# One DMA queue, a guard time behind each transfer, and another home for the attention outputs in a fused window-attention and SwiGLU kernel

## The chip, the cores and the metric

The kernel runs on one core of one Trainium2 chip. The metric is the device time of one execution in microseconds (us), as the median of the runs shown. A profiled execution gives the trace; its own time is listed beside it. Engines: TensorE (PE; its weight loads are PEld), VectorE (DVE), ScalarE (ACT), GpSimd (POOL) and SyncE (SP). DMAs are issued by SP, and in this kernel also by ScalarE.

## What is computed

```python
xn = layernorm(x)                                   # x: 2048 x 512
q, k, v = split(xn @ wqkv)                          # 32 heads of 16
p = softmax(q @ k.T / 4, where 0 <= i - j < 256)    # a sliding window of 256 keys
s = (p @ v) @ wo
f = (silu(xn @ w_gate) * (xn @ w_up)) @ w_down      # inner width 1792
out = x + s * silu(f)
```

All tensors are fp32. The kernel computes each dense product as three products of split operands (high x high, high x low, low x high), so every weight and every activation is written twice, as a rounded high part and a low rest.

## The kernel before, in words

**Tiles and stages.** The 2048 tokens are four chunks (c) of 512. A chunk's x is normalised, transposed by TensorE (`x_turn`, line 356, for chunk 0; `xt_turn`, line 485, for the others) and split into `xn[c % 2]`, two sets of buffers that chunks use in turn. The dense work of a chunk is a list of units, each with a 256 KB or 192 KB weight tile that is loaded (tile `wr`), split by ScalarE (`wh`, line 439) and GpSimd (`wl`, line 443), and used by TensorE in two 64-row halves side by side (all at line 478): `Proj` (q and k of two head groups, out `a`), `Values` (`vp`), `GateUp` (`g` and `u`, 14 a chunk), `Down` (`d`, four quarters, two halves each) and `Wo`, the output projection (`s`, two halves). Attention goes by 32 units u of one chunk and four heads: q and k come back from DRAM (`load_qk`, line 928), `max_pair` (line 957) forms scores `b` whose row maxima VectorE takes (`m`, line 978), `max_turn` (line 998) transposes the maxima and ScalarE negates them (`ms`, line 1019), a DMA writes them into a row of the q tile (`put`, line 1025), and the scores `c` are formed again with that row as an extra term (line 1116), so that ScalarE's exponential (`p`, line 1078) needs no subtraction. GpSimd masks `p`, and `pv_visit` (line 1133) multiplies with v, which carries a column of ones for the denominator. The result `ev` is stored to DRAM (`od`).

**Denominators.** When two units of a head group are stored, `reciprocals` (line 854) reads the denominators back (`den<-od`), VectorE inverts them (line 866) and a DMA writes them to DRAM (`rd<-den`). `o_prep` (line 877) then loads the outputs (`o<-od`) and the broadcast reciprocals (`r<-rd`), multiplies on GpSimd and splits into `oh`, the input of `Wo`. Before the change these copies take four of the eight buffers of the hidden activations (`hidden`, line 639, given back when `Wo` is done at line 803); only the last chunk's go into x buffers. `o_prep` opens with the end of a `Down` quarter (lines 721 to 730, sets `o_open` and `h_open`).

**What sets the order.** The program is written out by a planner that runs while the kernel is built; on the chip every engine follows its own list in order and waits on semaphores. The planner keeps a clock for TensorE's two halves (`issue`, line 1307) and a queue of jobs for each of VectorE, ScalarE, GpSimd and SP (letters V, S, G, D). `do` (line 110) adds a job with its earliest time, cost and slack; `pump` (line 136) gives each engine, when it is free, the able job with the least due time. `dma` (line 118) is such a job: at most eight are in flight (`lanes`), the landing is reckoned as the queue's backlog at 230 KB a us (`stream_at`) plus LAND = 3.5 us, and `then` is called with that time, from which everything that uses the data is planned. A DMA with `own=True` is issued by ScalarE (`e="S"`) and reckoned to land SHORT = 2.8 us after its issue, whatever the backlog. These are `put` of `ms`, and `fetch` and `back` of `reciprocals`. The dense units stand in one list made by `dense_order` (line 1222); attention visits have due times in units of attention, s = work / PACE - LEAD with PACE = 17.6 us, and are put between dense products when due and ready (lines 1394 to 1441). A `Wo` unit whose s is below 8 (c + 1) + OUT counts as early (variable `late`, line 1264), and a `Proj` may then go ahead of it.

Of the kernel before, what the change touches and what calls it, by code (L numbers as in the profile page):

```python
# [38 lines left out]
PCAP = 7168  # L39
NSL = 14  # L40
NWB = 10
WSL = 4.0
SPARE = 3
LAG = 7
# [4 lines left out]
MM = 0.2315  # L49
PACE = 17.6  # L50
LEAD = 1.1
OUT = 2.0
STEP = 0.05
LAND = 3.5
SHORT = 2.8


@with_exitstack
def tile_window_attention_swiglu_gate(
# [55 lines left out]
    lanes = [0.0] * 8  # L115
    stream_at = [0.0]

    def dma(ready, fn, then=None, slack=0.5, kb=256, can=None, e="D", own=False):
        def begun_at(t):
            if own:  # L120
                done = t + SHORT
            else:
                stream_at[0] = max(stream_at[0], t) + kb / 230.0
                done = stream_at[0] + LAND
            lanes.append(done)
            lanes.pop(0)
            if then:
                then(done)

        do(e, ready, 0.5, fn, begun_at, slack, lambda: lanes[0] <= now[0] and (can is None or can()), 0.0)  # L130

# [348 lines left out]


    def xt_ready(c, k):
        return latest([*(normed.get((c, t)) for t in range(4)), bank_time(rb_free, 2)])

    def xt_turn(c, k):
# [93 lines left out]
    class GateUp(Stationary):  # L579
# [7 lines left out]

        def done(self, i, pb, t, free):
            c, fb = self.c, self.fb
            if i == 0:  # L590
                def tanh():
                    self.th = take(f"th{c}_{fb}")
                    self.y = take(f"y{c}_{fb}")
                    nc.scalar.activation(self.th, pb, AF.Tanh, scale=0.5)

                def one():
                    nc.vector.scalar_tensor_tensor(
                        self.y, self.th, 1.0, pb, op0=ALU.add, op1=ALU.mult
                    )
                    give(self.th)  # L600

                def after_one(t):
                    free(t)
                    self.ty = t

                do("S", t, 0.5, tanh, lambda t: do("V", t, 0.61, one, after_one), can=room(2))
                return

            def product():
                self.h = take(f"h{c}_{fb}")  # L610
                nc.vector.scalar_tensor_tensor(
                    self.h, self.y, 0.5, pb, op0=ALU.mult, op1=ALU.mult
                )
                give(self.y)
                hid[c, fb] = hidden(f"hh{c}_{fb}")

            def high():
                nc.scalar.activation(hid[c, fb][:, 0, :], self.h, AF.Copy)

            def low():  # L620
                hl = hid[c, fb]
                nc.gpsimd.tensor_tensor(hl[:, 1, :], self.h, f32(hl[:, 0, :]), op=ALU.subtract)
                give(self.h)

            def after_product(t):
                free(t)
                do("S", t, 0.52, high, after_high, 1.0)

            def after_high(t):
                do("G", t, 1.24, low, lambda t: hready.__setitem__((c, fb), t), 1.0)  # L630

            do("V", t, 0.61, product, after_product, can=lambda: self.ty is not None and len(slots) >= 1 and hfree)

    hid = {}
    hready = {}
    hfree = [f"hr{i}" for i in range(NHID)]
    htag = {}
# [67 lines left out]
    class Down(Moving):  # L705
# [15 lines left out]
        def ended(self):  # L721
            for f in range(self.f0, self.f1):
                hid_release(hid.pop((self.c, f)))
            for n in range(2):
                if self.q == 2 + n:
                    h_open.add((self.c, n))
                if self.q == (2 if self.c < NCH - 1 else 0):
                    o_open.add((self.c, n))
                    for k in range(2):
                        o_prep(self.c, 2 * n + k)  # L730


        def done(self, i, pb, t, free):
            c, q, hf = self.c, self.q, self.hf
# [36 lines left out]
    class Wo(Moving):  # L771
# [28 lines left out]
        def done(self, i, pb, t, free):  # L800
            c, hf = self.c, self.hf
            p2 = pb.rearrange("p (t n) -> p t n", t=2)
            if hf == 1 and i == 1 and c < NCH - 1:
                for k in range(KC):
                    hid_release(oraw.pop((c, k)))
            finish(c, hf, i, p2, t, free)

    xr = {}
# [34 lines left out]


    ot = {}
    oraw = {}
    oready = {}
    o_open = set()
    h_open = set()
    od_at = {}  # L850
    rd_at = {}
    begun = set()
# [1 line left out]
    def reciprocals(c, k):  # L854
        t = latest(od_at.get(8 * c + 2 * k + n) for n in range(2))
        if t is None:
            return
        hd = slice(8 * k, 8 * k + 8)
        box = []

        def fetch():
            box.append(sb(f"den{c}_{k}", [P, 32], F32, "den", 2))
            move(box[0], od[c, hd, DH, :].rearrange("h (a n) -> h a n", n=32), nc.scalar)

        def rec():
            nc.vector.reciprocal(box[0], box[0])

        def back():
            move(rd[c, hd].rearrange("h (a n) -> (h a) n", n=32), box[0], nc.scalar)

        def landed_back(t):
            rd_at[c, k] = t
            o_prep(c, k)

        dma(t + 0.5, fetch, lambda t: do("V", t + 0.5, 0.3, rec, lambda t: dma(t + 0.3, back, landed_back, 0.5, 16, e="S", own=True)), 1.0, 16, e="S", own=True)

    def o_prep(c, k):
        if (c, k // 2) not in o_open or (c, k) not in rd_at or (c, k) in begun:
            return
        begun.add((c, k))  # L880
        hd = slice(8 * k, 8 * k + 8)
        box = []
        last = c == NCH - 1

        def fetch_o():
            box.extend(take(f"{n}{c}_{k}") for n in "or")
            move(box[0], od[c, hd, :DH, :])

        def fetch_r():
            move(box[1], rd[c, hd, :].unsqueeze(1).to_broadcast([8, DH, TC]))  # L890

        def mul():
            nc.gpsimd.tensor_tensor(box[0], box[0], box[1], op=ALU.mult)
            give(box[1])

        def high():
            if not last:
                t = hidden(f"oh{c}_{k}")
                oraw[c, k] = t
                ot[c, k] = [t[:, s, :] for s in range(2)]  # L900
            else:
                ot[c, k] = [xn[(c - 1) % 2][s][:, k, :] for s in range(2)]
            nc.scalar.activation(ot[c, k][0], box[0], AF.Copy)

        def low():
            nc.gpsimd.tensor_tensor(ot[c, k][1], box[0], f32(ot[c, k][0]), op=ALU.subtract)
            give(box[0])

        def then_o(t):
            dma(now[0], fetch_r, then_r, 0.0, 500)  # L910

        def then_r(t):
            do("G", t, 1.24, mul, then_mul, 1.0)

        def then_mul(t):
            do("S", t, 0.52, high, lambda t: do("G", t, 1.24, low, lambda t: oready.__setitem__((c, k), t), 0.5), 0.5,
               lambda: last or ((c, k // 2) in h_open and hfree))

        dma(max(now[0], rd_at[c, k]), fetch_o, then_o, 0.5, 256, room(2 + (0 if last else SPARE)))

# [77 lines left out]
    def max_turn(u, r):  # L998
        if r == 0:
            mtp[u] = [*bank(rb_free, f"mt{u}"), None]  # L1000
        pb, tag, _ = mtp[u]

        def go():
            nc.tensor.matmul(
                pb[:MW, R * r : R * r + R], mts[u % 2][half(r), :], ident[half(r), half(r)],
                is_transpose=True, start=True, stop=True,
            )

        if r == 0:
            def after(t):  # L1010
                mtp[u][2] = t

            extra[0].append((128, go, lambda t: do("V", t, 0.09, lambda: handover(pb), after, -1.0)))
            return
        box = []

        def neg():
            box.append(sb(f"ms{u}", [16, P], F32R, "ms", 2))
            nc.scalar.activation(box[0], pb[:16, :P], AF.Copy, scale=-1.0)

        def after_neg(t):
            rb_free[tag] = t
            dma(t - 0.17, put, lambda t: ms_at.__setitem__(u, t), -3.0, 8, e="S", own=True)

        def put():
            move(qs[u % 3][48 : 113 : 64], box[0], nc.scalar)

        extra[1].append((128, go, lambda t: do("S", t, 0.25, neg, after_neg, -1.0)))


# [191 lines left out]
    def dense_order():  # L1222
# [8 lines left out]
        for c in range(NCH):  # L1231
# [12 lines left out]
            gu(2, 3)  # L1244
            if c:
                wos(c - 1)
            gu(4, 5)
            dn(c, 0)
            gu(6, 7, 8)
            dn(c, 1)  # L1250
            if c < NCH - 1:
                gu(9, 10, 11, 12)
# [9 lines left out]
        while timed or ffn:  # L1262
# [5 lines left out]
            elif late and early and s > 8 * early[0][1].c - 2.4:  # L1268
                timed.remove(early[0])
                u = early[0][1]  # L1270
            else:
                u = ffn.pop(0)
            order.append(u)
# [32 lines left out]

    def issue(r, cols):
        front[0] = max(front[0], clock[r])
        clock[r] = front[0] + cols * 0.000444 + 0.004

    def next_mm(r):
        if extra[r]:
# [167 lines left out]
```

## Time and profile before

| | before |
|---|---|
| runs | 898.25, 899.52, 896.02 us |
| median | 898.25 us |
| profiled execution: its own time | 894.56 us |
| its span | 892.8 us |
| mean granted TensorE clock | 0.987 |
| DMA traffic | 139.60 MB, mean 156 GB/s |

The span is the time from the first to the last instruction of the profiled execution. Busy times are sums over an engine; matmuls are pipelined, so a busy TensorE isn't TensorE at its peak, and what counts is where it waits and at what clock it runs. A row of waits reads: the engine and line that waited, what ended the wait, then total us, times and the longest. A row of the chain reads: start, length, what; the chain is followed back from the last instruction, at each step to what released it. SPq and ACTq are the instruction queues of SyncE and ScalarE, in which DMAs are issued. Names such as `q<-ms` mean a tile written from another.

### The profile page before, as it was taken

The numbers are of one execution on the slowest core, as the hardware profiler recorded it, in microseconds if no ns is written. First come the engines' busy times: TensorE is split into PE (matmuls) and PEld (weight loads), VectorE is DVE, ScalarE is ACT, GpSimd is POOL, SyncE is SP. The second block draws the span as 40 slices with busy tenths as digits, with TensorE's granted clock in tenths as the row PEclk, the third lists the DMA queues.
The fourth block names the chain that finished last, engine by engine and source line by source line (L and its number), as shares of the span: only waits on it lengthen the run. The fifth ranks groups of instructions, "written<-read, shape, count | busy, mean of one in ns | idle before, by whom it ended". The sixth has DMA issues, their size and how long they took to land.

```text
span 892.8 us, 29790 instructions
## 1 busy us (share of the span) xinstructions
PE 867.6 (97%) x11966; PEld 802.2 (90%) x11966; DVE 504.4 (56%) x1663; ACT 480.4 (54%) x948; POOL 626.4 (70%) x904
## 2 busy tenths in 40 slices
PE   9999999999999799999899999999999999999997
PEld 8899888998899798989899989989899999998897
DVE  4454476654755466666547676566655576544234
ACT  3455465655655346655466546655655574555531
POOL 4766386858676567867678678757768697878780
PEclk9999999999999999999989999999999999999999
DMA  7765757467657873676748887385666866843441
GB/s 191 172 167 134 184 121 190 120 174 169 173 134 181 243 177 84 145 168 134 208 97 194 189 185 197 89 208 112 155 150 178 190 151 176 207 125 106 112 117 48
DMA packets 69485, 139.60 MB, mean 156 GB/s; under 512 B 14546, under 2 KB 23250, under 8 KB 69348
## 3 DMA queue, kind: packets, MB, share of 16 engines
q1 hardware_dynamic: 64004, 136.39, 63.1%
q8 instruction: 94, 1.54, 0.8%
q10 hardware_dynamic: 5344, 1.31, 0.8%
q14 instruction: 43, 0.35, 0.2%
HBM read 107.74 MB, written 29.62 MB: 154 GB/s over the span
## 4 chain that ended last, share of the span: by engine, by line
PE 82%; DMA 13%; DVE 1%; issue 1%; POOL 1%; SPq 1%; ACT 1%; ACTq 0%; DVEq 0%; POOLq 0%
PE d L478 16%; PE u L478 15%; PE g L478 15%; PE a L478 11%; PE pv L1153 7%; PE c L1116 5%; PE s L478 4%; PE b L970 4%; PE vp L478 4%; DMA q<-ms 3%; DMA q<-qkd 2%; DMA den<-od 2%; DMA wr<-wgu 2%; DMA xt<-x 1%; DMA qkd<-qkh 1%; PE warm L240 1%
## 5 line engine op out<-in xcount | busy, mean ns | idle before, releaser
L443 POOL TENSOR_TENSOR wl<-wr,wh 128x512 fp32r<-128x512 f32 (+3 forms) x262 | 310.5, 1200 | 73.5 <-ACT wh L439 63.8
L978 DVE CUSTOM_DVE_ANT_0 jk<-b,maskb 128x384 bf16<-128x384 f32 (+2 forms) x512 | 271.7, 531 | 125.2 <-PE b L970 61.0
L1078 ACT ACTIVATE p<-c 128x512 f32<-128x512 f32 (+2 forms) x384 | 198.6, 569 | 154.2 <-PE c L1116 133.1
L478 PE MATMUL d<-wh,hh 64*128 64x256 f32 x1792 | 266.8, 278 | 0.0
L478 PEld LDWEIGHTS d<-wh,hh 64*128 64x128 f32 x1792 | 229.4, 185 | 1.4 <-issue 0.6
L478 PE MATMUL d<-wl,hh 64*128 64x256 f32 x896 | 207.0, 277 | 0.0
L439 ACT ACTIVATE wh<-wr 128x512 fp32r<-128x512 f32 (+3 forms) x262 | 144.9, 591 | 38.4 <-POOL wl L443 8.2
L478 PE MATMUL g<-xh,wl 64*128 64x512 f32 x448 | 165.1, 399 | 0.0
L478 PE MATMUL g<-xh,wh 64*128 64x512 f32 x448 | 164.8, 400 | 0.0
L478 PE MATMUL g<-xl,wh 64*128 64x512 f32 x448 | 164.7, 399 | 0.0
L478 PE MATMUL u<-xl,wh 64*128 64x512 f32 x448 | 164.6, 399 | 0.0
L478 PE MATMUL u<-xh,wl 64*128 64x512 f32 x448 | 164.4, 399 | 0.0
L478 PE MATMUL u<-xh,wh 64*128 64x512 f32 x448 | 164.2, 398 | 0.0
L1090 POOL TENSOR_SCALAR_AFFINE_SELECT p<-p 128x256 f32<-128x256 f32 x256 | 102.0, 411 | 82.4 <-ACT p L1078 81.9
L478 PEld LDWEIGHTS d<-wl,hh 64*128 64x128 f32 x896 | 148.5, 185 | 0.4
L970 PE MATMUL b<-k,q 48*128 48x384 f32 (+2 forms) x512 | 121.0, 333 | 6.5 <-ACT p L1078 4.0
L1094 POOL TENSOR_SCALAR_AFFINE_SELECT p<-p 128x256 f32<-128x256 f32 x224 | 92.3, 412 | 37.9 <-ACT p L1078 36.6
L1116 PE MATMUL c<-q,k 49*128 49x128 f32 (+2 forms) x704 | 108.2, 305 | 8.8 <-DMA q<-ms 8.7
L1116 PEld LDWEIGHTS c<-q,k 49*128 49x128 f32 x704 | 88.2, 190 | 12.9 <-issue 8.1
L478 PE MATMUL a<-xh,wh 64*128 64x512 f32 x256 | 97.2, 396 | 0.1
L478 PE MATMUL a<-xh,wl 64*128 64x512 f32 x256 | 96.6, 395 | 0.0
L478 PE MATMUL a<-xl,wh 64*128 64x512 f32 x256 | 96.4, 394 | 0.0
(116 smaller groups left out, 2088.4 us busy)
## 6 DMA issues: line engine op xcount, KB each, us to landing
wr<-wgu SPq DMA_DIRECT2D x112, 256.0 KB
k<-qkd SPq DMA_DIRECT2D x48, 192.0 KB
wr<-wqk SPq DMA_DIRECT2D x32, 256.0 KB
qkd<-qkh SPq DMA_DIRECT2D x32, 256.0 KB
qkd<-qkl SPq DMA_DIRECT2D x32, 256.0 KB
q<-qkd SPq DMA_DIRECT2D x64, 128.0 KB
wr<-wdn SPq DMA_DIRECT2D x32, 256.0 KB
od<-ev SPq DMA_DIRECT2D x32, 256.0 KB
```

Of the source, the lines that this page charges most:

```text
L240: nc.tensor.matmul(wbank[:, : rhs.shape[-1]], warm, rhs, start=True, stop=True)
L439: nc.scalar.activation(wtile[j][0][pr, a:b], raw[pr, a:b], AF.Copy)
L443: nc.gpsimd.tensor_tensor(lo[pr, a:b], raw[pr, a:b], f32(hi[pr, a:b]), op=ALU.subtract)
L478: return nc.tensor.matmul(pb, a, b, start=first, stop=last, skip_group_check=True)
L970: nc.tensor.matmul(pb[:, :n], qs[u % 3][r : r + 48, p, qb * P : (qb + 1) * P], ks[u % 3][r : r + 48, p, lo : lo + n], start=True, stop=True,)
L978: nc.vector.tensor_tensor_reduce(junk[:, :n], pb[:, :n], maskb[:, 3 * P - n :], 1.0, -3.0e38, ALU.add, ALU.max, m[:, col : col + 1],)
L1078: nc.scalar.activation(t[:, h, :], pc[:, :n], AF.Exp, scale=DH ** -0.5)
L1090: nc.gpsimd.affine_select(s, s, [[0, 2], [1, P]], ALU.is_ge, 0.0, base=0, channel_multiplier=-1)
L1094: nc.gpsimd.affine_select(s, s, [[0, 2], [-1, P]], ALU.is_gt, 0.0, base=0, channel_multiplier=1)
L1116: nc.tensor.matmul(pc[:, at0 : at0 + w], ks[u % 3][r : r + 49, p, k0 : k0 + P], qs[u % 3][r : r + 49, p, qb * P : qb * P + w], start=(i == ...
L1153: nc.tensor.matmul(pbs[r][0][32 * j : 32 * j + 32, q0:q1], vt[half(r), (4 * c + kb) % VT, VW * (4 * g + j) : VW * (4 * g + j) + 32], t[hal ...
```

## The change

- `dma` loses `own` and SHORT: every DMA after the first x loads is issued by SP and reckoned with the common backlog. `reciprocals` and `put` lose their ScalarE issues.
- `then` of a DMA gets its landing time plus GUARD = 1.5 us, once the landing lies past 15 us. The lanes are still freed at the time without it.
- The attention outputs of every chunk c before the last go into `xn[c % 2]`, the x buffers of the chunk itself, once its last gate-up unit is done (`x_used`); the transposes of chunk c + 2 wait for `Wo` of chunk c (`x_free`). The last chunk's still go into the other set. No hidden buffers are taken, and `h_open` and `oraw` are gone.
- `o_prep` opens at gate-up unit OPEN = 11 (4 in the last chunk) instead of at the end of a `Down` quarter.
- Order: gate-up unit 6 goes ahead of the first `Down` quarter; OUT is 2.4 instead of 2.0; and where a `Wo` is early, the gate-up unit behind its two halves may go ahead of it.
- The planner reckons a 512-column product at 0.2339 us instead of 0.2313.

```diff
+OPEN = 11
-OUT = 2.0
+OUT = 2.4
-SHORT = 2.8
+GUARD = 1.5
...
-    def dma(ready, fn, then=None, slack=0.5, kb=256, can=None, e="D", own=False):
+    def dma(ready, fn, then=None, slack=0.5, kb=256, can=None, e="D"):
         def begun_at(t):
-            if own:
-                done = t + SHORT
-            else:
-                stream_at[0] = max(stream_at[0], t) + kb / 230.0
-                done = stream_at[0] + LAND
+            stream_at[0] = max(stream_at[0], t) + kb / 230.0
+            done = stream_at[0] + LAND
             lanes.append(done)
             lanes.pop(0)
             if then:
-                then(done)
+                then(done + (GUARD if t > 15.0 else 0.0))
...
     def xt_ready(c, k):
+        if c not in x_free:
+            return None
...
             c, fb = self.c, self.fb
+            if i == 1 and fb == FB - 1:
+                x_used.add(c)
+            if i == 0 and fb == (OPEN if c < NCH - 1 else 4):
+                o_open.add(c)
+                for k in range(KC):
+                    o_prep(c, k)
...
+    x_used = set()
+    x_free = {0, 1}
...
                 hid_release(hid.pop((self.c, f)))
-            for n in range(2):
-                if self.q == 2 + n:
-                    h_open.add((self.c, n))
-                if self.q == (2 if self.c < NCH - 1 else 0):
-                    o_open.add((self.c, n))
-                    for k in range(2):
-                        o_prep(self.c, 2 * n + k)
...
-            if hf == 1 and i == 1 and c < NCH - 1:
-                for k in range(KC):
-                    hid_release(oraw.pop((c, k)))
+            if hf == 1 and i == 1:
+                x_free.add(c + 2)
...
-            move(box[0], od[c, hd, DH, :].rearrange("h (a n) -> h a n", n=32), nc.scalar)
+            move(box[0], od[c, hd, DH, :].rearrange("h (a n) -> h a n", n=32))
...
-            move(rd[c, hd].rearrange("h (a n) -> (h a) n", n=32), box[0], nc.scalar)
+            move(rd[c, hd].rearrange("h (a n) -> (h a) n", n=32), box[0])
...
-        dma(t + 0.5, fetch, lambda t: do("V", t + 0.5, 0.3, rec, lambda t: dma(t + 0.3, back, landed_back, 0.5, 16, e="S", own=True)), 1.0, 16, e="S", own=True)
+        dma(t, fetch, lambda t: do("V", t, 0.3, rec, lambda t: dma(t, back, landed_back, 0.5, 16)), 1.0, 16)
...
-        if (c, k // 2) not in o_open or (c, k) not in rd_at or (c, k) in begun:
+        if c not in o_open or (c, k) not in rd_at or (c, k) in begun:
...
         def high():
-            if not last:
-                t = hidden(f"oh{c}_{k}")
-                oraw[c, k] = t
-                ot[c, k] = [t[:, s, :] for s in range(2)]
-            else:
-                ot[c, k] = [xn[(c - 1) % 2][s][:, k, :] for s in range(2)]
+            ot[c, k] = [xn[(c - last) % 2][s][:, k, :] for s in range(2)]
...
-               lambda: last or ((c, k // 2) in h_open and hfree))
+               lambda: last or c in x_used)
...
-            dma(t - 0.17, put, lambda t: ms_at.__setitem__(u, t), -3.0, 8, e="S", own=True)
+            dma(t, put, lambda t: ms_at.__setitem__(u, t), -3.0, 8)
...
-            move(qs[u % 3][48 : 113 : 64], box[0], nc.scalar)
+            move(qs[u % 3][48 : 113 : 64], box[0])
...
-            gu(4, 5)
+            gu(4, 5, 6)
             dn(c, 0)
-            gu(6, 7, 8)
+            gu(7, 8)
...
+            elif late and isinstance(ffn[2], GateUp):
+                u = ffn.pop(2)
             else:
                 u = ffn.pop(0)
...
-        clock[r] = front[0] + cols * 0.000444 + 0.004
+        clock[r] = front[0] + cols * 0.000453 + 0.002
```

More of the change, by code (lines that the diff above doesn't have):

```diff
@@ L845, in tile_window_attention_swiglu_gate @@
     ot = {}
-    oraw = {}
     oready = {}
     o_open = set()
-    h_open = set()
     od_at = {}
```

## The prediction

> **What bounds the kernel now.** I read the page's totals first, then TensorE's own waits, then the granted clock around them, then the chain through the gaps.
>
> ```profile
> span 892.8 us, 29790 instructions
> PE 867.6 (97%) x11966; PEld 802.2 (90%) x11966; DVE 504.4 (56%) x1663; ACT 480.4 (54%) x948; POOL 626.4 (70%) x904
> ```
>
> TensorE is the bound: 97% busy, with every other engine at 70% or less. Its work is not changed by the diff (same matrix products, another order), so the change can only win or lose time in which TensorE waits or runs at a lower clock. TensorE's waits, all of them over 0.15 us after the start-up (columns: total us, times, longest):
>
> ```profile
> PE c L1116 <- DMA q<-ms: 8.7, 5, 3.1
> PE b L970 <- ACT p L1078: 4.0, 2, 3.3
> PE b L970 <- DVE m L978: 2.4, 2, 2.1
> PE mt L1004 <- DVE m L978: 2.0, 1, 2.0
> PE s L478 <- issue: 1.7, 1, 1.7
> ```
>
> These add to 8.7 + 4.0 + 2.4 + 2.0 + 1.7 = 18.8 us. The second cost stands in the clock column of the windows (PEclk, third from the right):
>
> ```profile
> 309.70:316.50 6.80, 5.44 (x30) 4.78 (x32) 3.07 (x10) 3.29 (x6) 3.50 (x6) 0.50 0.74 194
> 446.20:453.00 6.80, 5.75 (x40) 5.78 (x42) 1.73 (x5) 1.68 (x3) 3.05 (x5) 0.50 0.96 202
> 524.70:528.10 3.40, 3.40 (x29) 3.40 (x27) 1.82 (x5) 1.09 (x2) 0.75 (x3) 0.50 0.91 186
> 695.40:698.80 3.40, 3.40 (x21) 3.40 (x19) 0.15 (x1) 1.52 (x5) 2.43 (x5) 0.50 0.71 201
> ```
>
> TensorE ran 6.8 + 6.8 + 3.4 + 3.4 = 20.4 us at half clock, which costs half of that, 10.2 us. Where do the waits come from? The chain, in order of time (start, length, what):
>
> ```profile
> 280.33 7.62 DMA q<-qkd
> ...
> 288.02 5.12 DMA q<-ms
> ...
> 441.41 5.71 DMA q<-ms
> ...
> 447.25 0.91 PE c L1116 x4
> ...
> 521.83 1.83 issue
> ...
> 795.41 9.03 DMA den<-od
> ```
>
> All but the one at 521.83 end in small transfers that ScalarE (ACT) issues: the negated row maxima (ms into q) and the softmax denominators (den); their reciprocals (rd) are the third kind. c starts 0.13 us after its ms has landed (441.41 + 5.71 = 447.12). den landed 9.03 us after its issue, at 804.44; VectorE (DVE) waits for it to form the reciprocals, and the row maxima m, for which b and mt wait, stand behind on VectorE. ScalarE is in order, so a DMA that cannot be issued yet also holds the exponentials behind it:
>
> ```profile
> 303.39 1.15 ACT L439 ACTIVATE wh<-wr 128x512 fp32r<-128x512 f32 x2
> 309.18 0.64 ACTq L98 DMA_DIRECT2D den<-od  x1
> 309.92 1.09 ACT L1078 ACTIVATE p<-c 128x512 f32<-128x512 f32 x2 [5.38 <-DMA xt<-x]
> ...
> 437.73 0.27 ACT L1019 ACTIVATE ms<-mt 16x128 fp32r<-16x128 f32 x1 [0.42 <-PE g L478]
> 441.41 0.52 ACTq L98 DMA_DIRECT2D q<-ms  x1
> ```
>
> From 304.54 to 309.18, 4.6 us, ScalarE did nothing but wait to issue the denominators; the exponentials came at 309.92, and TensorE waited for them (the 3.3 us of b for p). At 438.00 the maxima were ready, issued 3.4 us later and landed 5.7 us after that. Each time the planner had counted on 2.8 us after the issue (SHORT) and not on the traffic of the other queue.
>
> **The change part by part.** *All DMAs on SP.* ScalarE loses these issues (instruction, count, min/median/max in ns):
>
> ```profile
> L98 ACTq DMA_DIRECT2D q<-ms x32: 505/530/1142, 52.8 to 811.8; - x32
> L98 ACTq DMA_DIRECT2D den<-od x16: 627/632/640, 108.3 to 843.2; - x16
> L98 ACTq DMA_DIRECT2D rd<-den x16: 320/321/353, 114.2 to 849.5; - x16
> ```
>
> 32 x 0.53 + 16 x 0.63 + 16 x 0.32 = 32 us of issuing, plus the holds. ScalarE is busy 54%, so the 32 us are worth nothing by themselves; the holds are. The wait of b for p (4.0 us) goes, and the half-clock stretch at 309.7 behind it (6.8 us, so 3.4). SP takes the 32 us, and has room on average, as its own waits show:
>
> ```profile
> SPq L98 <- POOL wl L443: 107.8, 38, 8.5
> ```
>
> For 107.8 us it stands only until GpSimd has freed a weight buffer. But SP is in order too and now takes the holds over: queued behind a waiting ms, den or rd are the weight loads and the next unit's q and k, and for those TensorE has no wait today.
>
> *Slack.* The planner now reckons with LAND + GUARD = 3.5 + 1.5 = 5.0 us for these transfers plus the backlog of the queue, where it had 2.8 and none. That moves the readers later in every engine's fixed order, which is what the waits of c for ms (8.7) and of DVE's m (2.4 + 2.0) lack: the ms transfers above took 5.1 and 5.7 us, the den transfer 9.0. For ms the allowance grows by 2.2 us and the longest wait is 3.1, so a leftover of 0.9 at most if the transfer itself keeps its length. It will not quite: in the same burst q<-qkd on SP took 7.6 us where ms on ACT took 5.1, 2.5 longer, and in the burst around 441 two of SP's issues lie 3.3 us apart, so a transfer that comes in between waits half of that on average, some 1.6:
>
> ```profile
> 440.09 0.47 SPq L98 DMA_DIRECT2D wr<-wdn  x1
> 443.38 0.34 SPq L98 DMA_DIRECT2D od<-ev  x1
> ```
>
> So the bounds of this term are all (13.1 us) and less than nothing (the transfer lengthens by 2.5, the issue by 1.6, the allowance by 2.2: each wait grows by 1.9, five times 9.5 us). The backlog that is now counted decides, since it is largest just where the waits are; I take 70%: 9.2 us. Of the half-clock stretches at 446 and 695 (3.4 + 1.7 us lost) likewise 70%, 3.6. Longer reckoning also lets attention fall behind in a burst; dense products fill TensorE meanwhile, and this cover exists until the dense work runs short at the end, which it doesn't (below).
>
> *Heads' outputs in the x buffers.* The copies wait for the chunk's last gate-up instead of for free hidden buffers; the transposes of chunk c+2 now wait for the output projection of chunk c. The windows of s, and of the transposes (line 496), hold the tightest case, chunk 0 and chunk 2 (busy us and count after the comma: PE first):
>
> ```profile
> 265.00:303.00 38.00, 23.67 (x192) 22.55 (x192) 2.96 (x8) 1.00 0.79 214
> 303.00:338.00 35.00, 0.00 (x0) 0.00 (x0) 0.90 0.71 159
> 338.00:359.00 21.00, 2.42 (x32) 2.31 (x32) 1.00 0.46 102
> ```
>
> All 192 products of chunk 0's projection are done by 303, the transposes start after 338: 35 us of slack. OUT going from 2.0 to 2.4 moves the projection by 0.4 x 17.6 = 7 us, so the new wait costs nothing; with the slack gone it would hold the next chunk's q, k and v, all of attention. *Reordering.* Gate-up units go ahead of a projection that is early; the bytes moved stay the same. It shifts the x reloads and output stores out of the burst after 270 us; I cost it at nothing, with a bound of two waits like those above either way (3.4 us). *The planner's matmul time* (0.2339 instead of 0.2313 us) moves no instruction's cost. *Start and tail* stay: before 15 us no slack is added, and the tail is dense work.
>
> ```profile
> 834.73 2.38 PE pv L1153 x93
> ...
> 857.09 15.44 PE d L478 x263
> ```
>
> The last attention product ends at 837, and the chain still runs through a dense down projection at 857: some 20 us of cover for an attention that falls behind.
>
> *Two rules of the Trainium skill.* The half-clock stretches at 446.2 and 524.7 begin while TensorE waits (until 447.25) and 1.0 us after a wait (521.83 + 1.83). The Trainium skill, "TensorE: Matmul & The Clock Gate", Part 1, says that the clock halves after a fully idle window of about 3.4 us. The trace agrees on the length of a stretch (3.4, or twice that) but not on the need for a whole idle window, since 1.8 us of waiting sufficed at 521.83. By that rule no shortened wait would cost clock, all 5.1 us would come back instead of 3.6, and the forecast would be 1.5 us lower. The second rule speaks against the change. The Trainium skill, "DMA: Bandwidth & Descriptors", Queues, rings and completion order, says that a DMA engine takes turns between the queues and works through each queue's ring in order, so a small transfer passes the bulk on a queue of its own and on SP's stands behind it. The trace agrees in sign (5.1 against 7.6 us); rival B below is what that would do.
>
> **Sum.** 4.0 + 3.4 (ScalarE's hold) + 9.2 + 3.6 (late small transfers) = 20.2 us won; less 3.4 for two new waits of the present mean (8.7 / 5 = 1.7) in the longer SP queue: 16.8. The wait of s (1.7, and 1.7 of clock) I leave: it is put down to issue, and no DMA or engine ends it. Profiled execution: 894.56 - 16.8 = 877.8 us (its span of 892.8 and 1.8 us around it). The median of the three runs shown is 898.25, 3.7 above the profiled one, so the forecast on that scale is **881 us**.
>
> **The rivals.** *A, slower: SP is held.* If TensorE runs later than planned by more than the guard, SP stands at ms or den while loads wait behind it, and weights come late, 64 new places for that. For it: in bursts SP has no spare issue slot (rows at 440 to 443), and a bulk transfer takes 7.6 us there. Against it: outside bursts the guard covers it, and what stands behind was planned later as well. It decides from the point where a hold exceeds the 2.2 us of added allowance. Price: one such place costs a wait of 3.4 us (as b's 3.3 today) plus 10.2 / 4 = 2.6 of clock, 6 us; at five bursts 30 us on top of the forecast: **911 us**. *B, no change: the waits only move.* ScalarE's 7.4 us are won, but each of the five ms waits grows by 1.9 us (9.5 us) as bounded above: +2.1, about **900 us**. *C, the best case:* all of 17.1 and 8.5 us: 25.6, **873 us**; it lies in the forecast's own spread.
>
> **How the numbers follow.** Forecast (with C): 0.63, its own range 869 to 892. A: 0.25, 900 to 920. B: 0.12, 894 to 902. The range for 8 in 10 runs from 866 (C with a slightly faster run) to 908, and leaves out A's upper half. About 0.5%, 4.5 us, is what a measurement of this kernel can tell from no change: faster 0.63, within 0.5% 0.11, slower 0.26.
>
> **What would show it.** In the changed profile ScalarE issues nothing after the first x loads, and no idle time of several us stands before p; if p is still late, the hold was not ScalarE's DMA. c's waits for ms fall below 3 us in sum and the clock shows one or two half stretches instead of four. In SP's waits, holds by den and ms stay under 2 us each. Against me would be: weights (wr) among TensorE's or ScalarE's longest waits, q<-ms transfers of 8 us and more with c behind them, x transposes of chunk 2 waiting for s, or a later last pv than 837 us with a tail that is no longer dense.

## The result, and the profile after

The changed kernel takes 864.94 us (median of 4 runs, 863.66 to 865.71) against 897.27 us of the kernel before beside it (4 runs, 896.02 to 899.52). The ratio is 0.9636, 95% interval 0.961 to 0.9661: 3.6% faster, 32 us. The direction was forecast, the size not: 881 us was predicted, and 864.94 lies just below the range that began at 866.

Page of the changed kernel: span, busy time by engine, the chain by engine.

```profile
span 862.8 us, 29913 instructions
PE 854.0 (99%) x11966; PEld 789.7 (92%) x11966; DVE 506.1 (59%) x1663; ACT 478.0 (55%) x948; POOL 627.2 (73%) x904
PEclk9999999999999999999999999999999999999999
PE 96%; DVE 1%; DMA 1%; issue 1%; POOL 0%; ACT 0%; SPq 0%; DVEq 0%; POOLq 0%
```

The matrix products are the same 11966. TensorE's waits in the changed kernel (the row of the start-up included):

```profile
PE g L476 <- issue: 1.9, 1, 1.9
PE warm L238 <- DVE warm L233: 1.1, 1, 1.1
PE mt L996 <- DVE m L970: 0.4, 1, 0.4
PE b L962 <- DVE m L970: 0.2, 1, 0.2
```

Of 18.8 us of waits, 2.5 are left (start-up not counted), none of them for a transfer, and no slice shows a lowered clock. The half clock at the very end of both kernels (the last 3 us) comes after TensorE's last product; it costs nothing and is left out here and below. The waits won are 18.8 - 2.5 = 16.3 us and the half clock 10.2, together 26.5 of the 30.0 us between the profiled spans (892.8 - 862.8). The other 3.5 us stand in no wait: TensorE's busy time fell from 867.6 to 854.0 us, by 13.6, which is 3.4 more than the half clock gives, for the same products. The medians are 32.3 us apart, 2.3 more than the profiled executions (894.56 and 864.50), since the kernel before ran faster under the profile than in its other runs.

SP's own waits in the changed kernel, two rows of that view:

```profile
SPq L99 <- ACT ms L1011: 30.8, 10, 6.8
...
SPq L99 <- DVE den L863: 28.0, 10, 5.6
```

So SP now stands for the maxima and for the reciprocals, 20 times and 58.8 us in all, at the longest 6.8. No wait of TensorE for a transfer comes of it. ScalarE's waits for weights shrank, from 7.2 + 5.1 us in the two largest rows of before to 4.8 in the largest row of after (two smaller ones there add 1.8):

```profile
ACT wh L439 <- DMA wr<-wgu: 7.2, 4, 2.0
ACT wh L439 <- DMA wr<-wqk: 5.1, 2, 4.4
```
```profile
ACT wh L437 <- DMA wr<-wqk: 4.8, 1, 4.8
```

### The profile page after: what moved, and what is told of

It reads as the page before. It is cut to its first block, busy times and chain, and to the rows that moved or that the text cites. A ratio compares the mean times of both kernels' runs of the same rounds, so it can differ in the third digit from the quotient of the medians.

```text
span 862.8 us, 29913 instructions
## 1 busy us (share of the span) xinstructions
PE 854.0 (99%) x11966; PEld 789.7 (92%) x11966; DVE 506.1 (59%) x1663; ACT 478.0 (55%) x948; POOL 627.2 (73%) x904
## 4 chain that ended last, share of the span: by engine, by line
PE 96%; DVE 1%; DMA 1%; issue 1%; POOL 0%; ACT 0%; SPq 0%; DVEq 0%; POOLq 0%
PE d L476 18%; PE u L476 18%; PE g L476 18%; PE a L476 11%; PE pv L1145 8%; PE s L476 6%; PE c L1108 6%; PE vp L476 5%; PE b L962 5%; PE warm L238 1%; DMA r<-rd 1%; PE xp L496 0%; DVE xt L297 0%; DVE jk L970 0%; PE mt L996 0%
## 5 line engine op out<-in xcount | busy, mean ns | idle before, releaser
L1070 ACT ACTIVATE p<-c 128x512 f32<-128x512 f32 (+2 forms) x384 | 196.6, 572 | 132.0 <-PE c L1108 124.1
L476 PE MATMUL g<-xh,wl 64*128 64x512 f32 x448 | 166.9, 394 | 1.9 <-issue 1.9
L476 PE MATMUL g<-xh,wh 64*128 64x512 f32 x448 | 167.9, 395 | 0.0
L476 PE MATMUL u<-xh,wh 64*128 64x512 f32 x448 | 167.7, 396 | 0.0
L476 PE MATMUL u<-xl,wh 64*128 64x512 f32 x448 | 167.0, 396 | 0.0
L476 PE MATMUL g<-xl,wh 64*128 64x512 f32 x448 | 166.8, 395 | 0.0
L476 PE MATMUL u<-xh,wl 64*128 64x512 f32 x448 | 166.2, 395 | 0.0
L628 POOL TENSOR_TENSOR hh<-h,hh 128x512 fp32r<-128x512 f32 x56 | 72.5, 1294 | 41.8 <-ACT hh L624 36.4
L1108 PE MATMUL c<-q,k 49*128 49x128 f32 (+2 forms) x704 | 102.4, 299 | 0.0
```

The lines of the kernel that those rows point to most:

```text
L476: return nc.tensor.matmul(pb, a, b, start=first, stop=last, skip_group_check=True)
L1070: nc.scalar.activation(t[:, h, :], pc[:, :n], AF.Exp, scale=DH ** -0.5)
L1108: nc.tensor.matmul(pc[:, at0 : at0 + w], ks[u % 3][r : r + 49, p, k0 : k0 + P], qs[u % 3][r : r + 49, p, qb * P : qb * P + w], start=(i == ...
```

## The experiments

Three theories. **Theory 1**: the reckoning did it; readers are planned behind the backlog and the guard, so they no longer meet a transfer that is still on its way. **Theory 2**: the issuing engine did it; ScalarE is no longer held. **Theory 3**: the freed hidden buffers and the order of units did it. The edits below are against the kernel named. Each series has its own runs of the kernel before beside it, with medians of 898.60, 892.64 and 894.54 us (897.27 beside the changed kernel); ratios are to those. The changed kernel was not run again in a series, so a difference to it of a few us, such as e1's, is less sure than one between two runs of one series, such as e3 and e4, e5 to e8, or e9 to e12.

### Series 1

**e1, no guard**, against the changed kernel:

```diff
-GUARD = 1.5
+GUARD = 0.0
```

> The changed kernel with GUARD = 0: nothing else differs. Theory 1 (the reckoning of the transfers, backlog plus guard, took the waits away): the waits of c for ms and of VectorE's m come back in part, 3 to 10 us of TensorE waits and one or two half-clock stretches, 872 to 885 us. Theory 2 (ScalarE's holds were the whole loss, the issuing engine counts): no change, 863 to 867 us. Theory 3 (the freed hidden buffers and the new order of units smoothed the bursts): no change, 863 to 868 us.

868.25 us, ratio 0.9696 (0.9648 to 0.9744). Waits of c for ms come back, and are small:

```profile
PE c L1108 <- DMA q<-ms: 1.6, 3, 0.7
```

No half-clock stretch. The guard is worth some 3 us: less than theory 1 said (7 us or more), a little above what the others said. TensorE's other waits in e1 add up to 5.4 us, where the changed kernel has 2.5 in all, so the 1.6 for ms are not the whole of it. With e3 below, it is the backlog that counts, and not the guard.

**e2, issued by ScalarE**, against the changed kernel; the reckoning stays:

```diff
-            dma(t, put, lambda t: ms_at.__setitem__(u, t), -3.0, 8)
+            dma(t, put, lambda t: ms_at.__setitem__(u, t), -3.0, 8, e="S")
...
-            move(qs[u % 3][48 : 113 : 64], box[0])
+            move(qs[u % 3][48 : 113 : 64], box[0], nc.scalar)
```

and the same for `fetch` and `back` of `reciprocals`.

> The changed kernel with the 64 small transfers issued by ScalarE again, but reckoned as in the changed kernel (common backlog, LAND and GUARD). Theory 1: most of the gain stays, some holds of ScalarE come back, 866 to 874 us. Theory 2: the loss comes back, 885 to 900 us, with exponentials waiting behind DMAs. Theory 3: 864 to 870 us.

876.82 us, ratio 0.9794 (0.9735 to 0.9854): between the two expectations. TensorE's waits, then ScalarE's timeline at the longest of them, then the window of the only half-clock stretch:

```profile
PE c L1108 <- ACT p L1070: 6.4, 1, 6.4
PE b L962 <- ACT p L1070: 2.0, 1, 2.0
...
PE c L1108 <- DMA q<-ms: 0.6, 1, 0.6
```
```profile
389.01 0.62 ACT L600 ACTIVATE th<-g 128x512 f32<-128x512 f32 x1
397.65 0.63 ACTq L99 DMA_DIRECT2D den<-od  x1
398.32 1.08 ACT L1070 ACTIVATE p<-c 128x512 f32<-128x512 f32 x2 [8.69 <-DMA r<-rd]
```
```profile
395.10:405.30 10.20, 6.31 (x42) 6.13 (x44) 1.90 (x6) 2.80 (x5) 3.49 (x7) 0.50 0.76 178
```

From 389.63 to 397.65 ScalarE stood before a den transfer that could not be issued. That one hold cost 6.4 us of waiting and half of 10.2 of clock, 11.5 us in all. A second hold before a den transfer, from 294.99 to 299.29, is the 2.0 us of b for p. By the profiles, e2 has 9.2 us of waits where the changed kernel has 2.5, and 5.1 of clock: 11.8 us, which is the whole distance of the spans (874.6 - 862.8). The waits for ms stay gone (0.6). So the reckoning takes the ms waits, and moving the issue takes ScalarE's holds.

**e3, SP and backlog, no guard, old homes, old order**, against the kernel before:

```diff
-            dma(t - 0.17, put, lambda t: ms_at.__setitem__(u, t), -3.0, 8, e="S", own=True)
+            dma(t, put, lambda t: ms_at.__setitem__(u, t), -3.0, 8)
```

and the same for `reciprocals`, with SP's `move`.

> The kernel before with the small transfers issued by SP and reckoned with LAND and the common backlog, no guard, old homes and old order. Theory 1: half of the gain or less, 878 to 890 us, waits of c for ms remain. Theory 2: nearly all of the gain, 865 to 872 us. Theory 3: little gain, 885 to 897 us.

870.39 us, ratio 0.9725 (0.9669 to 0.978): 28 us below the 898.60 of the kernel before beside it, without guard, homes or order. Theory 1 had said half of the gain or less; the time is the one that theory 2 named, and e5 and e6 below tell whether the engine or the backlog gave it. One ms wait is left that matters:

```profile
PE c L1116 <- DMA q<-ms: 4.2, 2, 3.5
```

**e4, as e3 with the guard** (`then(done + (GUARD if t > 15.0 else 0.0))`, GUARD = 1.5).

> The kernel before with the small transfers on SP, and with GUARD = 1.5; old homes of the attention outputs, old order of units, old matmul time of the planner. Theory 1: nearly all of the gain, 865 to 872 us. Theory 2: as without the guard, 865 to 872 us. Theory 3: little gain, 880 to 897 us.

874.13 us, ratio 0.9756 (0.9709 to 0.9804). No wait for a transfer is left and the clock never drops, and yet the run is not faster than e3, and slower than theories 1 and 2 expected. The windows 266 to 275 of e4, then of the changed kernel (PE busy and its count first):

```profile
266.00:275.00 9.00, 9.00 (x71) 8.01 (x68) 4.97 (x16) 5.82 (x11) 7.25 (x11) 1.00 0.70 233
```
```profile
266.00:275.00 9.00, 9.00 (x96) 8.16 (x96) 6.78 (x24) 4.35 (x8) 4.56 (x11) 1.00 0.85 214
```

TensorE counts as fully busy in both, with 71 products in one and 96 in the other. A few microseconds of e4 (267 to 270) show what that is: one product every 0.23 us, where the changed kernel starts one in each half of the array.

```profile
267.04 0.39 PE L479 MATMUL a<-xh,wh 64*128 64x512 f32 x1
267.27 0.39 PE L479 MATMUL a<-xl,wh 64*128 64x512 f32 x1
```
```profile
267.46 0.39 PE L476 MATMUL g<-xh,wh 64*128 64x512 f32 x1
267.46 0.39 PE L476 MATMUL a<-xh,wl 64*128 64x512 f32 x1
267.70 0.39 PE L476 MATMUL a<-xh,wh 64*128 64x512 f32 x1
267.70 0.39 PE L476 MATMUL g<-xl,wh 64*128 64x512 f32 x1
```

One half of the array is empty. The next products of that half are chunk 0's output projection; with the guard its inputs are planned later than its turn (tried in e7 and e10). The first products of that projection, in e3 and then in e4, which differs by the guard alone (count, min/median/max in ns, first and last start):

```profile
L478 PE MATMUL s<-wh,oh x384: 272/277/412, 267.4 to 738.4; 64*128 64x256 f32 x192
```
```profile
L479 PE MATMUL s<-wh,oh x384: 272/276/389, 271.0 to 738.4; 64*128 64x256 f32 x192
```

The guard moved them from 267.4 to 271.0 us. By the profiles it took 4.2 us of waits away (6.0 in e3, 1.8 in e4, start-up not counted) and made TensorE 7.0 us longer busy (863.4 against 856.4 us) with the same products. In e3 the stretch is not half empty: counted in columns, TensorE runs 75 products of 512 columns from 266 to 275 us there, 47 in e4 and 76 in the changed kernel. The 28 that e4 lacks against e3 are some 3.3 us of a full array (an estimate from these counts).

### Series 2

**e5, SP alone**, against the kernel before: the issues go to SP, the reckoning stays SHORT (`own=True` without `e="S"`).

> The kernel before with the small transfers issued by SP, but still reckoned with SHORT = 2.8 us and no backlog: the issuing engine alone. If the issuing engine decides (ScalarE's holds): 868 to 876 us. If the reckoning decides: c waits for ms and VectorE for den at least as before (SP's ring is longer), 885 to 905 us, with no exponentials held behind a DMA.

885.67 us, ratio 0.988 (0.9806 to 0.9953). TensorE's waits, then the longest two ms transfers in the chain of e5, then the same unit's at 142 in the chain of before (the other, 5.71 at 441.41, stands in the prediction):

```profile
PE c L1116 <- DMA q<-ms: 12.5, 7, 4.3
```
```profile
146.02 8.76 DMA q<-ms
...
439.67 8.40 DMA q<-ms
```
```profile
142.64 6.06 DMA q<-ms
```

No exponential waits behind a DMA any more, and in exchange each of these two transfers is 2.7 us longer on SP (8.76 against 6.06, 8.40 against 5.71) and the waits for ms grow from 8.7 to 12.5 us. This is rival B's mechanism, seen where the reckoning is missing; its price is smaller than B's 9.5 us.

**e6, the reckoning alone**, against the kernel before: ScalarE issues, GUARD and backlog as in the changed kernel.

> The kernel before with ScalarE still issuing the small transfers, but reckoned with the common backlog, LAND and GUARD: the reckoning alone. If the reckoning decides: 872 to 882 us, waits of c for ms below 3 us, one or two holds of ScalarE left. If the issuing engine decides: 888 to 898 us.

889.21 us, ratio 0.9964 (0.9942 to 0.9987). The time is the one expected if the issuing engine decides; but the ms waits are small as theory 1 has it, and the time is lost elsewhere. TensorE's first waits, then the windows around the longest half-clock stretch:

```profile
PE c L1117 <- DMA q<-ms: 2.8, 2, 2.0
PE c L1117 <- ACT p L1079: 2.8, 1, 2.8
```
```profile
267.00:274.20 7.20, 6.67 (x35) 4.86 (x32) 4.13 (x12) 3.14 (x7) 3.24 (x7) 1.00 0.79 223
274.20:287.80 13.60, 13.60 (x86) 13.46 (x88) 2.38 (x9) 3.96 (x8) 7.60 (x11) 0.50 0.73 206
```

Again the half-empty array before chunk 0's projection, and this time 13.6 us at half clock behind it. So e6 does not measure the reckoning by itself: with the guard and the old order it brings a loss of its own. A run with ScalarE, the backlog and no guard was not made.

**e7, e4 with the new order of units** (OUT = 2.4, gate-up 6 moved, the `ffn.pop(2)` lines).

> SP, the guard, and the new order of units with OUT = 2.4, but the attention outputs still in hidden buffers and the planner's old matmul time. If the half-filled stretch of TensorE at 266 to 275 us of the run without the new order (output projection planned before its inputs are there) is the order's, it goes, and the time falls from 874 to 868 to 871 us; what is left to 865 is then the x buffers' or the matmul time's. If the x buffers cause it: 873 to 876 us.

867.31 us, ratio 0.9684 (0.9625 to 0.9743), 7 us below e4, a little more than expected if the stretch is the order's. From 266 to 275 us TensorE runs 94 products, close to the 96 of the changed kernel. **e8, the changed kernel with the old matmul time** (`cols * 0.000444 + 0.004`), differs from e7 only in the homes of the attention outputs and in OPEN.

> The changed kernel with the planner's old matmul time (0.2313 us for 512 columns): TensorE is then 1% slower than planned throughout. If the accuracy of that time matters: 868 to 875 us, SP held more often for ms and den. If it doesn't: 863 to 867 us.

864.40 us, ratio 0.9651 (0.9593 to 0.971): the matmul time is worth nothing here, and homes with OPEN 2.9 us at most. Neither run has a wait for a transfer or half clock; e7 has two waits put down to issue, 3.3 us, which e8 has not, so even the 2.9 need not be the homes' own:

```profile
PE s L479 <- issue: 2.0, 1, 2.0
PE vp L479 <- issue: 1.3, 1, 1.3
```

### Series 3

By now **theory 1b**: issue on SP and the longer reckoning are both needed; **theory 1c**: the longer reckoning needs the new order.

**e9, the changed kernel with the small transfers reckoned by SHORT** (still on SP, the guard stays for the others):

```diff
+            if own:
+                done = t + SHORT
...
-            dma(t, put, lambda t: ms_at.__setitem__(u, t), -3.0, 8)
+            dma(t - 0.17, put, lambda t: ms_at.__setitem__(u, t), -3.0, 8, own=True)
```

> The changed kernel (SP, new order, x buffers, guard on the bulk transfers) with only the small transfers reckoned as before, SHORT = 2.8 us after the issue and no backlog. Theory 1b (the reckoning and the issuing engine are both needed): 872 to 882 us, c waiting 6 to 15 us for ms as in the run with SP and SHORT alone. Rival (on SP, with the new order, the reckoning no longer matters): 864 to 868 us.

881.08 us, ratio 0.9854 (0.9807 to 0.9901): 16 us lost by the reckoning of the three small transfers, the first row of TensorE's waits being

```profile
PE c L1112 <- DMA q<-ms: 9.0, 3, 4.8
```

The time is the one that theory 1b has.

**e10, the changed kernel with the old order of units** (OUT = 2.0 and the two edits of `dense_order` undone).

> The changed kernel with the old order of units (OUT = 2.0, gate-up 6 behind the Down quarter, no gate-up ahead of an early output projection). Theory 1c (the longer reckoning needs the new order): 870 to 878 us, no DMA waits, but a half-filled stretch of TensorE before chunk 0's output projection near 270 us. Rival (order is worth nothing, the x buffers carry it): 864 to 867 us.

875.75 us, ratio 0.9803 (0.9753 to 0.9852). TensorE's longest wait after the start-up, the windows of e10, then one of the changed kernel:

```profile
PE b L962 <- DMA o<-od: 0.6, 1, 0.6
```
```profile
264.00:271.40 7.40, 7.13 (x42) 5.50 (x39) 3.98 (x12) 5.50 (x11) 6.01 (x7) 1.00 0.69 233
271.40:278.00 6.60, 6.57 (x31) 5.74 (x31) 2.41 (x9) 3.84 (x7) 5.50 (x11) 0.50 0.70 253
278.00:285.10 7.10, 7.10 (x53) 7.10 (x53) 0.31 (x2) 0.00 (x0) 0.91 (x1) 0.50 0.79 168
```
```profile
264.00:271.40 7.40, 7.40 (x74) 6.54 (x72) 4.91 (x18) 4.48 (x9) 2.44 (x7) 1.00 0.72 208
```

42 products against 74, then 13.7 us at half clock (6.9 lost). Theory 1c holds for the changed kernel as it stands, guard included. It does not hold for the counted backlog alone: e3 has that with the old order, starts its projection at 267.4 us and takes 870.39. What needs the new order is the guard, as e3 against e4 showed; e10 without the guard was not run.

**e11, the kernel before with the new order alone.**

> The kernel before with the new order of units alone. Theory 1c: no gain, 888 to 899 us, since with the short reckoning the output projection's inputs are there in time and the small transfers' waits stay. Rival (the order takes the bulk out of the burst after 270 us and with it the waits): 876 to 886 us.

888.61 us, ratio 0.9929 (0.9896 to 0.9962), its runs between 883.03 and 895.84. Less than 1%: a small gain where 1c said none, at the fast end of its range and above the rival's. The waits are the old ones: for ms 4.8 us, for p behind a den transfer 4.0, for m 2.7.

```profile
PE c L1116 <- DMA q<-ms: 4.8, 4, 1.7
PE c L1116 <- ACT p L1078: 4.0, 1, 4.0
PE mt L1004 <- DVE m L978: 2.7, 1, 2.7
```

**e12, the changed kernel with GUARD = 3.0.**

> The changed kernel with GUARD = 3.0, doubled. If a longer reckoning is free while dense work covers it: 863 to 867 us, no DMA waits. If it costs where a projection's inputs are planned too late: 868 to 878 us with half-filled stretches and no DMA waits.

880.26 us, ratio 0.9843 (0.9787 to 0.99): slower than both expectations. The one large wait of TensorE in e12, and VectorE's scalings of x (count, then min/median/max in ns):

```profile
PE u L476 <- DVE ho L473: 6.5, 1, 6.5
```
```profile
L297 DVE TENSOR_SCALAR xt<-xt,nm,rs x10: 533/551/9233, 12.3 to 527.0; 128x512 f32<-128x512 f32 x10
```

One scaling that takes 0.55 us elsewhere took 9.2, and TensorE stood for a hand-over behind it. By the profiles e12 has 4.8 us more of waits than the changed kernel and 3.4 of clock behind this one (526.0 to 532.8), 8.2 of the 16.1 us between the spans; the other 7.9 stand in neither. The half-filled stretch of the second expectation is there too, before chunk 0's projection, which starts at 287.3 us where the changed kernel has 281.9:

```profile
284.00:287.30 3.30, 3.30 (x33) 3.30 (x31) 0.69 (x1) 2.64 (x5) 1.80 (x3) 1.00 0.85 174
```

Until 287.3 these are products of 256 columns one at a time, one every 0.11 us; then the projection's run beside them. A half-filled array for 3.3 us is some 1.7 us lost (an estimate); where the rest of the 7.9 lies was not separated. So a larger guard is no free reserve, and it is not shown that the slow scaling is its doing.

## Why the prediction was wrong, point by point

- *What bounds the kernel, and the causes of the waits*: the causes are right (only the chain's first row, q<-qkd, is a transfer of SP's). The waits that the prediction named are gone with the change or down to 0.4 us, but for that of s (below), and e2, e5 and e9 bring the two kinds back one at a time: ScalarE's holds with the issue (6.4 + 2.0 us and 5.1 of clock in e2), the ms waits with the reckoning (12.5 us in e5, 9.0 in e9). **One step of it failed**: that the same products, in another order, "can only win or lose time in which TensorE waits or runs at a lower clock". TensorE's busy time itself moved, by 3.4 us beyond the clock in the changed kernel and by 7.0 from e3 to e4, where half of the array stood empty for a while.
- *ScalarE's hold, 4.0 + 3.4 us*: right, all of it went. What held it stands in the traces too. All DMAs of both queues take eight completion semaphores in turn, so that a small transfer on ScalarE can wait for an earlier bulk transfer of SP's to land: the maxima ready at 438.00 shared their semaphore with the store in this row of the chain of before, which lands at 441.33, and were issued at 441.41. The den transfer issued at 309.18 shared its own with a weight load of SP's that was issued at 300.20 and landed at 309.11.

```profile
431.02 10.31 DMA qkd<-qkh
```

- *The slack, "I take 70%: 9.2 us"* and 3.6 of clock: **this term was mis-sized.** 13.1 us became 0.6, and the two stretches (5.1 us) became none: 17.6 instead of 12.8. The transfers do get longer on SP, 2.7 us measured in two of them (e5) against the 2.5 estimated; that the two agree is partly luck, since the estimate set a larger load of q against the 8 KB of ms. The counted backlog covers it. The bound "each wait grows by 1.9 us", 9.5 in all, was not reached even without the reckoning: in e5 the waits for ms grew by 3.8 us in sum.
- *"Less 3.4 for two new waits in the longer SP queue"*: **mis-sized too**, it is nothing. SP is held up to 6.8 us, where the prediction's sign had under 2, and far beyond the 2.2 us from which rival A was to decide; yet no load came late for TensorE: what stands behind was planned later as well, the argument that the prediction gave against A and did not trust.
- *The wait of s and the clock at 524.7* (1.7 + 1.7): left standing; the clock came back, and the wait of that kind moved to a g (1.9 us).
- *Reordering, "I cost it at nothing", bound 3.4 us*: **wrong.** Without it the changed kernel takes 10.8 us more (e10). The prediction looked for its effect in the burst after 270 us. It lies in the guard: that plans the projection's inputs later, and the old order leaves half of the array empty before them (e3 against e4). The prediction's cover, "dense products fill TensorE meanwhile", exists, with the guard, because of the reordering (e4 against e7).
- *x buffers, matmul time*: right at nothing, within the 2.9 us that e7 and e8 are apart.
- *Sum and scale*: 30.0 us instead of 16.8 by the profiles. The two mis-sized terms are 4.8 + 3.4, the clock of s 1.7, less 0.2 for the wait that moved to g: 9.7 of the 13.2 missing. The other 3.5 are the time that stands in no wait, a term that the prediction did not have; it lies in TensorE's busy time, and which stretches give it was not separated. So even the best case C, 25.6 us, was exceeded. Then the scale: the forecast added the 3.7 us by which the median of before lay above its profiled execution, and the changed kernel's median lies only 0.4 above its own. These 3.3 us and the 13.2 make 16.5, the distance from 881.45 (898.25 - 16.8) to 864.94.
- *The two rules of the Trainium skill*. The one of the Trainium skill's "DMA: Bandwidth & Descriptors", Queues, rings and completion order, by which a small transfer stands behind the bulk on SP's queue, spoke against the change and agrees with e5 (8.76 against 6.06 us). It costs nothing here once the plan counts the backlog. The one of the Trainium skill's "TensorE: Matmul & The Clock Gate", Part 1, by which the clock halves after an idle window, would have had all 5.1 us of clock come back; they did, but the waits themselves went too, so this does not test it. e10 (from 271.4 us on, with no wait above 0.6) and e6 (from 274.2 on) halve the clock without a long wait before it, so a missing wait is no proof of a full clock.

What stays open: where the rest of the 7.0 us lies by which TensorE is longer busy in e4 than in e3, beyond the 3.3 of the half-empty stretch, and what of the 2.9 us between e7 and e8 is the homes'. Every edit also writes out a new plan, and part of a difference of a few us can be an accident of the new plan, as e12's slow scaling may be; e8's new plan took the time of the changed kernel within 0.6 us, but no series of plans that differ in nothing else was run.

## What to carry to other kernels

When a plan is written out ahead, a transfer's landing has to be reckoned with the traffic of the queue that it stands in; which engine issues it decides who is held when the plan is wrong, and here the engine with compute work behind it was the wrong one. The two belong together: the issue alone gave 1.2% (e5), the reckoning alone 0.4% (e6, guard included), issue and backlog together 2.7% (e3) of the 3.6%. A guard on top, which plans readers later still, paid only where other work was put in their place, so guard and order are one change: the guard with the old order did not pay (e4), and the order alone gave 0.7% (e11). And read a full engine by its products per window, not by its busy share: the half-empty array was 100% busy.

## What the runs showed of the hardware

- In e10 the clock halved for 13.7 us although TensorE's longest wait was 0.6 us: in the microseconds before, it had worked with one half of the array (until 269.7 us) and then on attention products alone. The prediction had tied half clock to waits. A half-empty array by itself did not do it: e4 kept the full clock in the same stretch, with little more work and no gap. The rows are of e10, then of e4; where between them the clock gives way is not shown.

```profile
268.00:271.40 3.40, 3.13 (x19) 2.21 (x17) 1.74 (x6) 2.15 (x5) 3.32 (x3) 1.00 0.57 207
```
```profile
268.00:271.40 3.40, 3.40 (x22) 2.80 (x22) 0.78 (x2) 2.27 (x4) 2.66 (x4) 1.00 0.86 278
```

- The VectorE instruction of 0.55 us stood for 9.2 in e12 while GpSimd was busy for 9.77 of the 10 us (fifth busy time in the window's row), and ended 0.3 us after GpSimd's last instruction of that burst. That the two engines hinder each other is a guess from this one place; it was not tried.

```profile
517.00:527.00 10.00, 4.74 (x48) 4.43 (x44) 10.00 (x5) 6.44 (x13) 9.77 (x19) 0.95 0.84 225
```

- Kernels with such waits spread more from run to run: 883.03 to 895.84 us in ten runs of e11 against 863.66 to 865.71 in four of the changed kernel.
